# Folding weights in column quarters, loading q, k and v apart, the last tile in halves, and one more batch's q and k transposed by DMA

## Chip, cores and metric

One core of one Trainium2 chip runs the whole program. The metric is the device time of one execution in microseconds (us). The kernel before took 204.28 us (median of 3 runs, 203.37 to 205.15) when the change was proposed, and 204.2 to 204.9 us in every later group of runs.

## The reference

Windowed attention with four sink positions, then a multiplicative feed-forward layer over the 3072 tokens:

```python
# q, k, v: (4, 8, 768, 64) fp32; n_sink = 4, window = 128
scores = q @ k.T / sqrt(64)
keep   = (key < n_sink) | (0 <= query - key < window)
attn   = softmax(where(keep, scores, -1e9)) @ v
x      = attn.transpose(0, 2, 1, 3).reshape(3072, 512)
out    = ((x @ w1) * (x @ w2)) @ w3 @ w_out     # w1, w2: 512x1024, w3: 1024x1024, w_out: 1024x512
```

## The kernel before

The product w3 @ w_out ("the fold", `w3o`) is computed once at the start, while the first loads arrive. Each of the four batches then goes through the same stages: load q, k, v (GpSimd's queue, cast to bf16), transpose q and k, scores, softmax, values, gates (`pg`, the matmuls with w1 and w2), projection (`po`) and store. Batches overlap. The instruction order on TensorE, ScalarE, VectorE and SP is fixed when the program is built, by a small list scheduler inside the kernel which models when each load arrives; GpSimd's order is chosen by the framework.

```python
XPOSE   = (2, 3)        # batches whose q and k are transposed by DMA; 0 and 1 by TensorE
X_XPOSE = (2, 3)        # the same for x
...
qN = per_batch("qN", [P, NB, DM], 2)      # two buffers: batch 3's q overwrites batch 1's
kN = per_batch("kN", [P, NB, DM], 2)
vN = per_batch("vN", [P, NB, H, VS], 3)   # VS = 72
...
def load_qkv(b, kb):                      # one 128-row block: k, q, v in turn
    for src, dst in ((k, heads(kN[b][:, kb, :])), (q, heads(qN[b][:, kb, :])),
                     (v, vN[b][:, kb, :, 0:D])):
        nc.gpsimd.dma_start(out=dst, in_=rows(src, b, kb))
...
def transposes(src, dst, t):              # TensorE: 8 matmuls and a VectorE copy
    ...
def transposes_dma(src, dst, kb):         # SP's queue
    nc.sync.dma_start_transpose(out=dst[:, :, kb * P:(kb + 1) * P], in_=src[:, kb, :])
...
def project(b, m):
    po = ps_mm.tile([P, DM], FP32, tag="mm", name="po")
    ...                                   # 8 matmuls of 512 columns
    o_sb = work.tile([P, DM], FP32, tag="o_sb", name="o_sb")     # pool of 3 buffers
    nc.scalar.copy(o_sb[:], po[:])
    nc.sync.dma_start(out=out[t0:t0 + P, :], in_=o_sb[:])        # SP's queue too
...
# scheduler's constants
MARGIN = {"av": 0.3}; YIELD = {..., "sc": 0.4, ...}
PACE = 5.0              # least us of the model's time between two units of scores
```

The softmax here doesn't subtract the row's maximum and nothing guards it: scores larger than these inputs give would overflow.

## Time and profile before

| | before |
|---|---|
| time, span of the profiled run | 203.94 us, 202.2 us |
| granted TensorE clock | 1.000 |
| first gate matmul | 39.57 us |
| TensorE's waits of over 0.45 us after that | none |
| last matmul ends, tail to the end of the span | 198.6 us, 3.6 us |
| chain of work that ended last | PE 87%, DMA 7% |

A wait is time in which an engine stands idle in front of an instruction; the profile writes it in brackets behind that instruction, with what ended it. TensorE (PE) ends this kernel, so its waits are what matters, and those of other engines only if they come through to it. The prediction shows the page's lines and reads them.

### The profile page before, as it was taken

How to read it: one execution, taken by the hardware profiler on the slowest of the kernel's cores; microseconds unless marked ns; L12 is line 12 of the kernel's file. 1: busy time of each engine (PE TensorE's matmuls, PEld its weight loads, DVE VectorE, ACT ScalarE, POOL GpSimd, SP SyncE). 2: the span in 40 equal slices, each digit the busy share in tenths (PEclk: the TensorE clock that was granted, in tenths of full speed). 3: DMA queues.
4: the chain of work that ended last, by engine and by line, in shares of the span. 5: the costliest groups of instructions: out<-in, count | busy, mean ns of one | idle time of the engine just before them, and what ended most of it. 6: DMA issues, size and time to landing. Idle time of an engine off the chain costs nothing.

```text
span 202.2 us, 4514 instructions
## 1 busy us (share of the span) xinstructions
PE 192.7 (95%) x1800; PEld 120.7 (60%) x1813; DVE 109.9 (54%) x263; ACT 107.0 (53%) x180; POOL 74.1 (37%) x97
## 2 busy tenths in 40 slices
PE   7949899999999999999999999999999999999992
PEld 2425466698886885576666655566665466554440
DVE  4613288665897773467878654877775044440000
ACT  2231556755765866777666664666663433333331
POOL 6699494488999963622770000000000000000000
PEclk9999999999999999999999999999999999999999
DMA  5999999999999999999999994502021610002333
GB/s 154 294 219 173 165 197 206 192 156 154 154 150 151 161 144 126 214 175 204 155 132 157 118 161 129 159 5 52 3 52 67 192 55 2 0 3 104 150 145 120
DMA packets 102773, 27.04 MB, mean 134 GB/s; under 512 B 95072, under 2 KB 98144, under 8 KB 102752
## 3 DMA queue, kind: packets, MB, share of 16 engines
q0 software_dynamic: 78624, 13.64, 91.5%
q1 hardware_dynamic: 24128, 13.11, 29.9%
q8 instruction: 14, 0.23, 0.5%
q14 instruction: 7, 0.06, 0.1%
HBM read 29.36 MB, written 6.29 MB: 176 GB/s over the span
## 4 chain that ended last, share of the span: by engine, by line
PE 87%; DMA 7%; ACT 2%; issue 1%; DVE 1%; SPq 1%; ACTq 0%
PE pg L316 42%; PE po L362 19%; PE av L276 7%; PE sc L245 6%; DMA ab_106<-in_moe_w_dram 5%; PE pw L351 3%; PE tp L191 2%; PE ph L351 2%; DMA xT_104<-xn 2%; PE xt L292 1%; PE pz L376 1%; PE sp L226 1%; ACT w3o L355 1%; SPq L140 1%; ACT w_sb L163 1%
## 5 line engine op out<-in xcount | busy, mean ns | idle before, releaser
L316 PEld LDWEIGHTS <-w_sb 128*128 128x128 bf16 x576 | 53.0, 98 | 25.5 <-issue 1.6
L323 ACT COPY a_sb<-pg 128x384 f32<-128x384 f32 (+1 forms) x72 | 32.0, 445 | 35.2 <-PE pg L316 15.0
L250 ACT ACTIVATE ex<-sc 128x1024 bf16<-128x1024 f32 (+1 forms) x48 | 44.8, 955 | 7.6 <-PE sc L245 7.0
L254 DVE TENSOR_TENSOR am<-ex,maskt 128x1024 bf16<-128x1024 bf16 (+1 forms) x48 | 30.3, 641 | 4.4 <-ACT ex L250 4.2
L366 ACT COPY o_sb<-po 128x512 f32<-128x512 f32 x24 | 14.1, 586 | 26.9 <-PE po L362 26.7
L316 PE MATMUL pg<-xT_102,w_sb 128*128 128x256 bf16 x192 | 24.3, 273 | 0.0
L316 PE MATMUL pg<-xT_103,w_sb 128*128 128x384 bf16 x128 | 23.7, 326 | 0.0
L316 PE MATMUL pg<-xT_104,w_sb 128*128 128x384 bf16 x128 | 22.6, 326 | 0.4 <-DMA xT_104<-xn 0.4
L283 DVE TENSOR_TENSOR xn<-av,rec 128x256 bf16<-128x256 f32 x48 | 20.4, 424 | 4.1 <-DMA xT_104<-xn 2.5
L316 PE MATMUL pg<-xT_105,w_sb 128*128 128x384 bf16 x128 | 21.0, 326 | 0.0
L276 PEld LDWEIGHTS <-am 128*128 128x128 bf16 x352 | 17.0, 97 | 3.3 <-issue 0.3
L320 DVE TENSOR_TENSOR ab_109<-a_sb,pg 128x384 bf16<-128x384 f32 x16 | 8.8, 553 | 17.1 <-PE pg L316 17.1
L280 DVE RECIPROCAL rec<-av 128x4 f32<-128x4 f32 x48 | 8.6, 180 | 16.5 <-PE av L276 16.2
L320 DVE TENSOR_TENSOR ab_106<-a_sb,pg 128x256 bf16<-128x256 f32 x24 | 10.0, 418 | 5.7 <-PE pg L316 4.2
L376 PE MATMUL pz<-ksbd_113 128*128 128x512 bf16 x36 | 10.5, 444 | 1.4 <-DVE ksbd_113 L146 1.3
L362 PE MATMUL po<-w3o,ab_106 128*128 128x512 bf16 x45 | 11.2, 379 | 0.2
L320 DVE TENSOR_TENSOR ab_108<-a_sb,pg 128x384 bf16<-128x384 f32 x16 | 8.9, 554 | 4.4 <-PE pg L316 1.6
L362 PE MATMUL po<-w3o,ab_107 128*128 128x512 bf16 x46 | 10.9, 379 | 0.1
L351 PEld LDWEIGHTS <-w3t 128*128 128x128 bf16 x64 | 6.0, 97 | 8.3 <-issue 2.0
L362 PE MATMUL po<-w3o,ab_108 128*128 128x512 bf16 x46 | 10.6, 379 | 0.1
L362 PE MATMUL po<-w3o,ab_109 128*128 128x512 bf16 x47 | 10.5, 379 | 0.1
L320 DVE TENSOR_TENSOR ab_107<-a_sb,pg 128x384 bf16<-128x384 f32 x16 | 8.8, 552 | 2.7 <-ACT ex L250 1.5
(143 smaller groups left out, 254.4 us busy)
## 6 DMA issues: line engine op xcount, KB each, us to landing
out_dram<-o_sb SPq DMA_DIRECT2D x24, 256.0 KB, 2.1
w_sb<-in_moe_w_dram POOLq DMA_DIRECT2D x5, 512.0 KB, 10.1
ab_106<-in_moe_w_dram SPq DMA_DIRECT2D x2, 512.0 KB, 7.5
w_sb<-in_moe_w_dram POOLq DMA_DIRECT2D x4, 256.0 KB, 8.3
ab_107<-in_moe_w_out_dram SPq DMA_DIRECT2D x2, 512.0 KB, 6.9
kN_86<-in_k_dram POOLq DMA_DIRECT2D x6, 128.0 KB, 8.8
qN_82<-in_q_dram POOLq DMA_DIRECT2D x6, 128.0 KB, 8.6
vN_90<-in_v_dram POOLq DMA_DIRECT2D x6, 128.0 KB, 8.5
```

The lines of the kernel that those rows point to most:

```text
L245: nc.tensor.matmul(sc[:, e, c:c + n], kT[b][hp, r, kb * P:(kb + 1) * P], qT[b][hp, r, qb * P:qb * P + n], start=True, stop=True)
L250: nc.scalar.activation(ex[:, :, c0:], sc[:, :, c0:], ACTF.Exp, scale=scale)
L254: nc.vector.tensor_mul(am[:, :, c0:], ex[:, :, c0:], mk)
L276: nc.tensor.matmul(o, lhs, rhs, start=(n == 0), stop=(n == len(todo) - 1), skip_group_check=True)
L283: nc.vector.tensor_mul(xns[b, t][:, :, r, :, :], av[:, :, :, 0:D], rec[:].to_broadcast([P, 2, 2, D]))
L316: nc.tensor.matmul(pg[:], w_sb[:, kk, dt * P:(dt + 1) * P], xT[b][:, kk, tk], start=(kk == 0), stop=(kk == NP - 1))
L320: nc.vector.tensor_mul(ab[b][:, dt, tk], gate_a.pop((b, c, dt))[:], pg[:])
L323: nc.scalar.copy(a_sb[:], pg[:])
L351: nc.tensor.matmul(po, w3T[i][:, j, :], wo_sb[:, j, :], start=(j == 0), stop=(j == KFF - 1))
L362: nc.tensor.matmul(po[:], ab[b][:, kk, m * P:(m + 1) * P], w3o[:, kk, :], start=(kk == 0), stop=(kk == KFF - 1))
L366: nc.scalar.copy(o_sb[:], po[:])
L376: nc.tensor.matmul(pz[:], idle[:, 0:P], idle[:, 0:512], start=True, stop=True)
```

## The change

The intent is to take work and waits off TensorE: start the fold sooner (in quarters, the first with both ScalarE and VectorE casting), put the first q, k and v where they are wanted, move batch 1's 48 transposing matmuls to DMA, and shorten the tail. The scheduler's constants were re-tuned along with it. Cut to its core:

```diff
-    XPOSE = (2, 3)
+    XPOSE = (1, 2, 3)
...
-    def load_qkv(b, kb):           # k, q, v of a block in turn
+    def load_heads(names, b, kb):  # "kq" or "v"
...
-    order = [('w3', 0, 2, 1, 2), ('w3', 2, 4, 1, 2), ('wo', 1), ('qkv', 0, 0, 2), ...
-             ('qkv', 1, 0, 6), ('qkv', 2, 0, 6), ('qkv', 3, 0, 6)]
+    order = [('wo', 4, 6), ('w3', 0, 2, 512), ('w3', 2, 4, 512), ('wo', 6, 8), ('qk', 0, 0), ...
+             ('qk', 2, 4), ('v', 3, 0), ('qk', 3, 0), ('qk', 3, 2), ('qk', 3, 4), ('v', 3, 2), ('v', 3, 4)]
...
-        for h in range(2 if i < SPLIT else 1):                       # fold in halves
+        parts = [(0, 2), (2, 4), (4, 6), (6, 8)] if i < SPLIT else [(0, KFF)]
...
+    def project_last():            # last tile: two halves of 256 columns, the second
+        ...                        # copied in quarters by VectorE and ScalarE, three stores
-                task(("av", b, r, t), 3, ...)
+                task(("av", b, r, t), 5, ...)
-                task(("p", b, m), 1300 + 200 * b + m, ...)
+                task(("p", b, m), 1380 + 200 * b + m, ...)
-    MARGIN = {"av": 0.3};  YIELD "sc": 0.4;  PACE = 5.0
+    MARGIN = {"av": 0.5};  YIELD "sc": 0.6;  PACE = 2.75
```

## The prediction

> **What bounds the kernel now.** I read the page's first two parts first, then the chain of work that ended last, then the DMA totals of single stretches, and last the timeline around the places that mattered.
>
> ```profile
> span 202.2 us, 4514 instructions
> ...
> PE 192.7 (95%) x1800; PEld 120.7 (60%) x1813; DVE 109.9 (54%) x263; ACT 107.0 (53%) x180; POOL 74.1 (37%) x97
> ...
> PE   7949899999999999999999999999999999999992
> ...
> DMA  5999999999999999999999994502021610002333
> ```
>
> The reader is to see two full rows. TensorE is busy throughout, DMA only to slice 24 or so, some 125 us. TensorE ends the kernel, so what counts is its useful work plus whatever it waits. The chain gives the real spacing of its matmuls (busy means include the pipeline and can't be added):
>
> ```profile
> 43.29 3.49 PE pg L316 x32
> 46.79 0.89 PE tp L191 x16
> ...
> 160.56 20.80 PE pg L316 x128
> 181.62 10.74 PE po L362 x49
> ```
>
> That is 0.109 us for a 256-column matmul, 0.055 for a 128-column one, 0.1625 for 384 and 0.217 for 512. Laying the program's order of TensorE out with these spacings (scores about 0.046 and values about 0.034 apiece, from the same chain) gives 179.9 us of useful work. It starts at 1.3 and ends at 198.6, so some 17.4 us are lost: about 14.5 before the first gate matmul at 39.6 (fillers and waits for loads), 1 before the first gate of batch 2, the rest in small pieces.
>
> The DMA row needs a rate. Two stretches, the first (42 to 57 us) with cast loads alone, the second (70 to 98) with loads, transposes and stores:
>
> ```profile
> q0 software_dynamic: 18023, 2.27, 248.9%
> ```
>
> ```profile
> q0 software_dynamic: 15563, 1.96, 118.1%
> q1 hardware_dynamic: 6836, 2.78, 64.3%
> ```
>
> A q, k or v load writes 0.131 MB, so the first stretch did 17.3 loads in 15 us: 0.87 us a load. In the second, 15 loads take 13.0 of 28 us; the hardware queue moved 5 stores (1.31 MB, about 0.75 us each, 3.7) and 1.47 MB of transposes, 11.2 of them, in the 11.3 us left: **1.0 us a transpose**. Between 98 and 130 us, 12 loads, 18 transposes and 3 stores make 31 of 32 us, which agrees. So DMA is a full server until about 125 us, and each item put in delays what is behind it.
>
> How late were the last batch's q and k?
>
> ```profile
> 98.19 1.19 SPq L200 DMA_TRANSPOSE kT_101<-kN_89  x1
> ...
> 123.98 0.50 PE L245 MATMUL sc<-qT_97,kT_101 64*128 64x256 bf16 x8
> ```
>
> The first transposes of batch 3 go out at 98.2 to 103.9, and their first reader runs at 124.0. Even with some 7 us to land they were early by more than 12 us. That slack is what the change spends.
>
> **What the Trainium skill says.** "DMA: Bandwidth & Descriptors", section "Queues, rings and completion order", says that an engine round-robins between the queue rows that have work. The trace agrees that loads and transposes share: a v load of batch 1 landed in 6.8 us with no transposes about, one of batch 3 in 15.4. The same page, "Issuing engine by pattern", gives plain DMA transposes to the hardware path (SP here): all stand in SP's queue, in order, behind each other and the stores. Its "Latency and other measured facts" has 261 GB/s for a transpose, which for 0.131 MB would be 0.5 us; this trace says 1.0 and I use that. "TensorE: Matmul & The Clock Gate", "The HAM clock gate", says an idle window of about 3.4 us halves the clock until some 3.4 us of work have passed. Before shows slow matmuls only at its start (0.43 us apart in place of 0.217); it has no later gap long enough to test it.
>
> **The change part by part.**
> *Batch 1 transposed by DMA.* Takes 48 transposing matmuls from TensorE: 48 x 0.055 = 2.65 us, on the bounding engine, and six VectorE copies of 0.69 us, which nobody waited for. The useful work becomes 177.3 us. Adds 12 transposes to DMA: 12 x 1.0 = 12 us, in a stretch where it is full.
> *Loads apart and reordered.* Up to the first w2 half (landed at 35.8 before: the load eight places later, which reuses its slot, goes out then) the new order has six more q, k, v loads: 35.8 + 6 x 0.9 = 41.2. But by the first gate TensorE has then 27.3 us of useful work behind it, against 23.8 at 39.6 before; the offset of the clock over work done is 13.9 in place of 15.8. The fold in quarters and the casts on two engines help there (fillers fall from 37 to 26): 1.9 us won at the front, if nothing waits later.
> *Last tile in halves.* Before, TensorE ends at 198.6 and the span at 202.2: a 0.59 us copy, a 256 KB store and the end. Now the last copies are 128 columns wide, on two engines, and the stores 64 KB: about 0.3 + 0.3 us saved. The tail becomes 3.0.
> Sum if nothing waits: 177.3 + 13.9 + 2.5 of small losses + 3.0 = **196.7 us** of span against 202.2, that is 198.6 us of time.
>
> *But the loads' order has a side that the diff doesn't show.* In the built program GpSimd's instruction order for batch 3 is v x2, k x6, v x4, then q x6: all q last (they overwrite q of batch 1, whose transposes now are DMAs that finish late, and the scheduler put the rest ahead). Before, k and q alternated. The first scores of batch 3 need two blocks of q transposed, and TensorE executes in order. When does the first q arrive? In both kernels all weights and batch 0 are in at about 46.8 (from the slot reuse; same bytes). After that come, ahead of or with that q: 49 loads (18 + 18 + 13), 12 + 12 transposes of batches 1 and 2, one k of batch 3 and two x transposes, six stores:
> 49 x 0.87 + 27 x 1.0 + 6 x 0.75 = 42.6 + 27 + 4.5 = 74.1; 46.8 + 74.1 = **120.9**.
> The same sum for before's first k of batch 3: 40 x 0.87 + 12 + 4.5 = 51.3, which gives 98.1; the trace issues its transpose at 98.19. So I trust the sum to a microsecond or two.
> SP's queue then holds q, k, q at about 1.3 us each, the second q going out at about 123.6, and landing takes 2.4 to 9 us in the trace for batch 3; with four loads still about I take 3.5: **127**. TensorE without waits would be there at 102.4 us of work + 13.9 + 1 = 117.3. It waits near 10 us. Then its x transposes for batch 2's gates stand in the same queue behind those: about 1.2 more. A 10 us gap would also cool the clock by what the skill says: about 1.5 more.
> The sum on the path: 127 + (177.3 - 102.4 = 74.9 of work; before took 74.6 us for 73.9, so + 0.7) + 1.2 + 1.5 + 3.0 = 208.3 us of span. Time is about 1.7 to 2 us over the span (203.94 profiled for 202.2): 210. Because I may have the landing and the cooling too high, I say **209**.
>
> **The rivals.**
> *The gain stands* (198 to 200 us): the transposes of batch 1 come from TensorE, DMA's extra 12 us hide. For it: DMA is idle from 130 us on, and before had over 12 us of slack. Against: the q loads move 9 loads (8 us) later on top of the 12, and TensorE gets there 5 us sooner.
> *A wash* (201 to 205): q arrives as I say but a shorter wait, with landing in 2.4 us and no cooling. It takes back just what the front and the 2.65 us won. This is close to my figure and can't be ruled out.
> *Stalls come earlier, too*: batch 2's third pair of transposes lands at about 110 by the same sums, TensorE wants it at about 107. It would not add: the wait at batch 3 is fixed by DMA, and swallows earlier ones.
> *The front gets worse* (fold in quarters with VectorE's memsets in between, raw loads in 1 KB rows): this too would be swallowed, as long as DMA runs as before. So the front hardly matters for the time, if I'm right.
>
> **Range and chances.** The sum has an error of 2 us at the arrival, 2 at the landing, 2 at the cooling: 209 with 203 to 214. Faster by over 2% means under 200.2 and needs the wait to be nearly absent: 0.08. Slower by over 2% is above 208.4: 0.55. Within: 0.37.
>
> **What would show it.** Right: one wait of TensorE of 7 to 12 us for the transposed q of batch 3 at the first scores of batch 3, ending at about 127; SP's transpose of that q held until 120 to 122; DMA's row full to about 140; first gates at about 41 us; about 75 to 78 us from those scores to TensorE's end; tail about 3.0 us; low clock spacing (0.3 us and more) just after the wait. Wrong: q and k of batch 3 in time (a wait under 3 us, and a span of some 197), which would mean that a transpose costs DMA much less than 1.0 us beside loads, or that something earlier on TensorE is the new limit.

## The result, and the profile after

The changed kernel took **210.62 us** (median of 4 runs, 209.94 to 213.54, the last of these in the slow state) against 204.38 (4 runs, 203.37 to 205.15). The ratio is 1.0297, with a 95% interval of 1.0228 to 1.0366: slower. The slow run is left out of the ratio. Ratios here are the mean time of one kernel's fast runs over that of the other's of the same rounds, so not quite the ratio of the medians quoted. The profiled run was fast, at 211.16 us.

The page of the changed kernel, its rows of busy tenths and its chain:

```profile
span 209.4 us, 4456 instructions
PE 191.0 (91%) x1747; PEld 117.8 (56%) x1762; DVE 108.4 (52%) x266; ACT 106.3 (51%) x181; POOL 75.2 (36%) x98
...
PE   7989998999999998699996977499999999999993
...
PEclk9999999999999999699999999999999999999999
DMA  6999999999999999999999995564202330001344
...
PE 52%; DMA 34%; POOL 5%; SPq 4%; issue 2%; DVE 2%; ACT 0%; ACTq 0%; DVEq 0%
```

TensorE's row, unbroken before, now has dents at slices 16, 21 and 23 to 25. A slice is 5.2 us, so these are at about 85, 112 and 120 to 135 us. In slice 16 the clock is low, too. The chain has become a third DMA. The DMA row is full to about 126 us, where it was to about 121 before, so it doesn't show the added work by itself; the last of all loads does, which GpSimd issues at 117.5 us instead of 103.8. TensorE's waits, longest first (total us, times, longest):

```profile
PE pg L324 <- ACT o_sb L374: 5.3, 2, 3.0
PE sc L253 <- DMA qT_97<-qN_85: 2.9, 1, 2.9
PE sp L234 <- DVE am L262: 2.1, 1, 2.1
```

There are four waits of over 2 us, 10.2 us together. TensorE's timeline places three of them (start, duration, instruction, and in brackets the idle time before it):

```profile
85.40 2.72 PE L324 MATMUL pg<-xT_103,w_sb 128*128 128x384 bf16 x8 [2.29 <-ACT o_sb L374]
...
127.18 0.51 PE L253 MATMUL sc<-qT_97,kT_101 64*128 64x256 bf16 x8 [2.91 <-DMA qT_97<-qN_85]
...
134.40 2.76 PE L324 MATMUL pg<-xT_104,w_sb 128*128 128x384 bf16 x16 [2.96 <-ACT o_sb L374]
```

The one at 127.18 is the first scores of batch 3. SP's queue just before it shows why, and also what stood behind:

```profile
110.51 1.21 SPq L208 DMA_TRANSPOSE kT_101<-kN_89  x1
121.80 1.19 SPq L208 DMA_TRANSPOSE qT_97<-qN_85  x1
...
130.02 0.34 SPq L377 DMA_DIRECT2D out_dram<-o_sb  x1
```

Between 111.7 and 121.8 SP issued nothing: the transpose of q at its head waited for a load. The store that left at 130.02 had its tile ready when ScalarE's copy ended at 120.4; it stood behind those transposes. ScalarE's timeline shows what that costs:

```profile
84.76 0.59 ACT L374 COPY o_sb<-po 128x512 f32<-128x512 f32 x1 [3.56 <-DMA out_dram<-o_sb]
...
133.76 0.59 ACT L374 COPY o_sb<-po 128x512 f32<-128x512 f32 x1 [4.64 <-DMA out_dram<-o_sb]
```

ScalarE stood 3.56 and 4.64 us until a store had landed: all three output buffers were full. As its copy did not come, the slot in PSUM (the memory into which TensorE writes) was not freed, and TensorE stood as well, 2.29 and 2.96 us. So the waits at 85 and 134 are waits for stores. The fourth, at 113.76 before `sp`, is put down to a VectorE tile, but `sp` also reads `qT_96`, batch 2's transposed q, whose third pair went out at 104.60 and landed at 113.67 by the trace, just before the wait ended.

Is a transpose still 1.0 us of DMA? From 98 to 121 us, when only loads and transposes moved (q0 are GpSimd's loads, q1 what SP issues; packets, MB, and the time that their packets took as a share of the 23 us in 16 engines, which can pass 100% as packets overlap):

```profile
q0 software_dynamic: 19404, 2.45, 186.9%
q1 hardware_dynamic: 3818, 0.92, 37.1%
```

2.45 MB are 18.7 loads of 0.131 MB, 16.3 us at 0.87 us each; 6.7 us are left for 7.0 transposes, 0.96 us each. The prediction's rate holds.

The tail: TensorE's last matmul, then the two last quarter copies.

```profile
204.08 1.91 PE L387 MATMUL po<-w3o,ab_109 128*128 128x256 bf16 x16
```

```profile
206.41 0.27 ACT L396 COPY o_sb<-po 128x128 f32<-128x128 f32 x1 [1.50 <-DVE o_sb L396]
```

VectorE's copy ran from 206.08 to 206.37, and only then did ScalarE's begin. They were meant to run side by side. The tail is 3.4 us.

### The profile page after: what moved, and what is told of

Same layout as the page of the kernel before. It is cut to its first block, busy times and chain, and to the rows that moved or that the text cites. A ratio compares the mean times of both kernels' runs of the same rounds, so it can differ in the third digit from the quotient of the medians.

```text
span 209.4 us, 4456 instructions
## 1 busy us (share of the span) xinstructions
PE 191.0 (91%) x1747; PEld 117.8 (56%) x1762; DVE 108.4 (52%) x266; ACT 106.3 (51%) x181; POOL 75.2 (36%) x98
## 4 chain that ended last, share of the span: by engine, by line
PE 52%; DMA 34%; POOL 5%; SPq 4%; issue 2%; DVE 2%; ACT 0%; ACTq 0%; DVEq 0%
PE pg L324 28%; PE po L370 11%; DMA vN_92<-in_v_dram 8%; DMA kN_88<-in_k_dram 7%; DMA qN_85<-in_q_dram 6%; DMA kN_89<-in_k_dram 4%; DMA qN_82<-in_q_dram 4%; PE av L284 3%; PE pw L359 3%; PE sc L253 3%; SPq L208 2%; DMA ab_106<-in_moe_w_out_dram 2%; POOL vN_92 L105 2%; DMA out_dram<-o_sb 2%; SPq L311 1%
## 5 line engine op out<-in xcount | busy, mean ns | idle before, releaser
L324 PEld LDWEIGHTS <-w_sb 128*128 128x128 bf16 x576 | 54.5, 98 | 31.0 <-issue 7.6
L262 DVE TENSOR_TENSOR am<-ex,maskt 128x1024 bf16<-128x1024 bf16 (+1 forms) x48 | 29.8, 641 | 3.6 <-ACT ex L258 3.5
L374 ACT COPY o_sb<-po 128x512 f32<-128x512 f32 x23 | 13.5, 587 | 31.9 <-PE po L370 22.3
L324 PE MATMUL pg<-xT_103,w_sb 128*128 128x384 bf16 x128 | 25.0, 339 | 2.3 <-ACT o_sb L374 2.3
L324 PE MATMUL pg<-xT_104,w_sb 128*128 128x384 bf16 x128 | 22.8, 326 | 3.0 <-ACT o_sb L374 3.0
L324 PE MATMUL pg<-xT_102,w_sb 128*128 128x256 bf16 x192 | 22.1, 273 | 0.0
L324 PE MATMUL pg<-xT_105,w_sb 128*128 128x384 bf16 x128 | 21.0, 326 | 0.1
L284 PEld LDWEIGHTS <-am 128*128 128x128 bf16 x352 | 16.2, 97 | 2.5 <-issue 0.8
L328 DVE TENSOR_TENSOR ab_109<-a_sb,pg 128x384 bf16<-128x384 f32 x16 | 8.9, 555 | 15.2 <-PE pg L324 15.2
L328 DVE TENSOR_TENSOR ab_106<-a_sb,pg 128x256 bf16<-128x256 f32 x24 | 10.1, 421 | 10.0 <-PE pg L324 9.8
L370 PE MATMUL po<-w3o,ab_106 128*128 128x512 bf16 x44 | 11.1, 379 | 0.2
L370 PE MATMUL po<-w3o,ab_107 128*128 128x512 bf16 x45 | 10.9, 379 | 0.2
L370 PE MATMUL po<-w3o,ab_108 128*128 128x512 bf16 x46 | 10.4, 379 | 0.1
L359 PEld LDWEIGHTS <-w3t 128*128 128x128 bf16 x64 | 5.4, 97 | 8.7 <-DVE w3t L345 4.0
L359 PE MATMUL ph<-wo_sb,w3t 128*128 128x512 bf16 x31 | 8.3, 380 | 1.6 <-DVE w3t L345 1.1
L405 PE MATMUL pz<-ksbd_113 128*128 128x512 bf16 x24 | 8.6, 508 | 1.3 <-DVE ksbd_113 L151 1.3
```

The lines of the kernel that those rows point to most:

```text
L262: nc.vector.tensor_mul(am[:, :, c0:], ex[:, :, c0:], mk)
L284: nc.tensor.matmul(o, lhs, rhs, start=(n == 0), stop=(n == len(todo) - 1), skip_group_check=True)
L324: nc.tensor.matmul(pg[:], w_sb[:, kk, dt * P:(dt + 1) * P], xT[b][:, kk, tk], start=(kk == 0), stop=(kk == NP - 1))
L328: nc.vector.tensor_mul(ab[b][:, dt, tk], gate_a.pop((b, c, dt))[:], pg[:])
L359: nc.tensor.matmul(po, w3T[i][:, j, :], wo_sb[:, j, :], start=(j == 0), stop=(j == KFF - 1))
L370: nc.tensor.matmul(po[:], ab[b][:, kk, m * P:(m + 1) * P], w3o[:, kk, :], start=(kk == 0), stop=(kk == KFF - 1))
```

## The experiments

The theory after the first look: DMA is the server that is behind; batch 1's transposes delay every later load, and TensorE pays in whatever it then asks for first. The rivals: it is the order of batch 3's loads alone; it is the stores behind transposes alone; it is the new pace, or the new front. All twelve profiled runs were in the fast state. Times are medians of all runs, ratios are of fast runs to the kernel before in the same rounds.

| run | what it is | us | ratio, 95% interval |
|---|---|---|---|
| after | the change | 210.62 | 1.0297 (1.0228 to 1.0366) |
| e1 | after, batch 1 transposed by TensorE | 206.37 | 1.0077 (1.0033 to 1.0122) |
| e2 | before, batch 1 transposed by DMA | 213.48 | 1.0456 (1.0410 to 1.0503) |
| e3 | after, k and q of batch 3 in turn | 206.32 | 1.0103 (1.0051 to 1.0155) |
| e4 | after, stores on ScalarE's queue | 221.26 | 1.0833 (1.0777 to 1.0888) |
| e5 | e1 with the old pace | 205.05 | 1.0012 (0.9989 to 1.0034) |
| e6 | after with the old pace | 217.23 | 1.0627 (1.0580 to 1.0674) |
| e7 | after, four output buffers | 209.41 | 1.0213 (1.0154 to 1.0272) |
| e8 | after, only k of batch 1 by DMA | 211.84 | 1.0368 (1.0328 to 1.0409) |
| e9 | after, 12 v loads left out (wrong result) | 200.67 | 0.9793 (0.9756 to 0.9831) |
| e10 | before, last tile in halves | 204.80 | 0.9996 (0.9976 to 1.0016) |
| e11 | e5 with four output buffers | 204.93 | 1.0005 (0.9985 to 1.0025) |
| e12 | e3 and e7 together | 205.03 | 1.0009 (0.9984 to 1.0035) |

### e1 and e2: the change without the transposes, and the transposes without the change

```diff
 # e1, on after                 # e2, on before
-XPOSE = (1, 2, 3)             -XPOSE = (2, 3)
+XPOSE = (2, 3)                +XPOSE = (1, 2, 3)
```

> The changed kernel, with q and k of batch 1 transposed on TensorE again (XPOSE back to batches 2 and 3); everything else of the change stays. Theory A (DMA is a full server; the twelve added transposes, and the place of batch 3's q behind all other loads, make TensorE wait for batch 3's q): without the twelve the waits of 2.1 and 2.9 us for transposed q, and the two waits of 2.3 and 3.0 us for an output buffer behind them, go; useful work rises by 2.65 us to 179.9. Span 179.9 + 14.5 (front) + 2.5 (small losses) + 3.3 (tail) = 200, time 202, ratio to before 0.98 to 0.995. Rival B (the new load order, pace and fold by themselves bring the waits): time stays above 207.

> The kernel before, with one part of the change alone: q and k of batch 1 transposed by DMA. Theory A: useful work falls to 177.3, but q and k of batch 3 come 12 us later; by the count of loads, transposes and stores ahead of them the first pair lands near 125 where TensorE would be ready at about 122: waits of 3 to 6 us in sum, span 203 to 206, time 205 to 208, ratio 1.00 to 1.02. Rival C (the transposes as such pay, the loss is from the rest of the change or from q being loaded last): below 202, ratio under 0.99.

Both directions came as expected and both sizes were missed. In e2 the transposes alone cost 4.6%, more than the whole change, although k and q of batch 3 are loaded in turn there: the order of these loads alone can't be the cause. Its longest wait, 3.26 us ending at 128.2, runs through yet another buffer: VectorE could not write its next x tile until a transposed x had landed.

```profile
127.13 0.42 DVE L283 TENSOR_TENSOR xn<-av,rec 128x256 bf16<-128x256 f32 x1 [5.28 <-DMA xT<-xn]
```

In e1 the four waits are gone, but a new one of 2.46 us stands at 119:

```profile
119.02 0.29 PE L234 MATMUL sp<-qT,ksbd 128*32 128x256 bf16 x4 [2.46 <-DMA qT<-qN]
```

The reason is in the program's order: with the new pace, and with a model that sees less DMA work, the scheduler puts batch 3's first scores after 94.6 us of TensorE work, where the kernel before has 106.0 and the changed one 102.4. Without the transposes the loads come earlier, and they are asked for earlier still. One more thing moved: in e1 (and e5) GpSimd loads k and q of batch 3 in turn again, so e1 holds e3's cure as well, and what it won can't be put down to the transposes alone.

### e3: only the order of batch 3's loads

```diff
-    for x in order[GATED:]:
-        load(*x)
+    with tc.manual_schedule(engines={mybir.EngineType.Pool}):
+        for x in order[GATED:]:
+            load(*x)
```

The built program differs in GpSimd's order for batch 3 alone, where k and q now alternate.

> The changed kernel with only the order of batch 3's loads put back to k, q, k, q (GpSimd's list held in written order); TensorE's, VectorE's, ScalarE's and SP's orders are the same, all twelve added transposes stay. Theory A: the second q of batch 3 is issued nine loads sooner, near 117 in place of 124; the wait at the first scores of batch 3 (2.9 us) goes, and the 3.0 us wait for an output buffer, whose store stands behind that q in SP's queue, goes too; the waits near 83 and 112 stay. Time 205 to 206, ratio to the changed kernel about 0.975. Rival D (only the sum of DMA work counts, not its order): within 1 us of the changed kernel.

206.32 us, just over the 205 to 206 of the theory and far from the rival. The first q of batch 3 is transposed at 112.09 instead of 121.80, and TensorE no longer waits for it:

```profile
112.09 1.22 SPq L209 DMA_TRANSPOSE qT<-qN  x1
```

```profile
123.97 0.50 PE L254 MATMUL sc<-qT,kT 64*128 64x256 bf16 x8
```

So "all q last" was 1.9 points of the 3.0 (1.0297 to 1.0103). The output-buffer wait that was to go with it only shrank, from 2.96 to 1.91 us. Left are 2.7 us for output buffers, 1.8 for v of batch 2 and 1.7 for q of batch 2.

### e4: the stores out of SP's queue

```diff
-        nc.sync.dma_start(out=out[t0:t0 + P, :], in_=o_sb[:])
+        nc.scalar.dma_start(out=out[t0:t0 + P, :], in_=o_sb[:])
```

> The changed kernel with the output stores (all but the last tile's) issued from ScalarE's queue in place of SP's; the scheduler then also puts batch 3's loads as k, q, k, q. Theory A with the part found in the trace (stores stuck behind transposes that wait for loads hold the three output buffers, ScalarE waits for a buffer, and TensorE for the PSUM slot that ScalarE empties): the waits of 2.3, 2.9 and 3.0 us go, the one of 2.1 us near 112 for q of batch 2 stays or grows to 4, since DMA sets it. Time 203 to 205. Rival: if ScalarE's issue time (0.3 to 0.4 us each, 23 times) delays its copies on the path, 206 or more.

A clear miss, 221.26 us, from one wait: TensorE stood 19.3 us before scores that needed ScalarE to empty earlier ones first (`ex`). ScalarE's timeline:

```profile
88.50 0.38 ACTq L377 DMA_DIRECT2D out_dram<-o_sb  x1
88.98 0.81 ACT L258 ACTIVATE ex<-sc 128x768 bf16<-128x768 f32 x1 [20.58 <-DMA kT<-kN]
```

ScalarE's last work before that ended at 68.4. It then stood in front of a store's issue until a transposed k had landed. The semaphores in the packed trace show why: the DMAs issued by SP and by ScalarE share eight completion semaphores. This store has number 115, as had the transpose of k that SP issued at 80.65 us, and ScalarE waited on 115 until that transpose landed, at 88.42. A queue that can be held does not become harmless by moving it onto a computing engine: the engine is then held with it. (The order of batch 3's loads changed along with it to k and q in turn, as expected.)

### e5 and e6: the old pace

```diff
-PACE = 2.75; MARGIN "av": 0.5; YIELD "sc": 0.6; av prio 5; p prio 1380
+PACE = 5.0;  MARGIN "av": 0.3; YIELD "sc": 0.4; av prio 3; p prio 1300
```

e5 is e1 with this edit, e6 is the changed kernel with it.

> The changed kernel without the transposes of batch 1 by DMA (as in e1) and also with the scheduling constants of the kernel before (pace of the score units 5.0 instead of 2.75, the old priorities of values and projections). Theory: what held e1 back was only the new pace, which asks for batch 3's scores before DMA can deliver them (its one wait of 2.46 us at 119); with the old pace they are wanted some ten us of work later, so no wait of over 1 us stands after 50 us, and the gain of front and tail (about 2 us at the front by my prediction) shows: 200 to 203 us, 0.98 to 0.995 of the kernel before. Rival (the new front and the split loads are no gain on this chip, whatever the pace): 204 or more.

> The changed kernel with its transposes of batch 1 by DMA kept, and the scheduling constants of the kernel before. Theory: the transposes of batch 1 are the cost and the pace only says where it shows; batch 3's scores are wanted later, so the wait that ended at 127.2 goes, but waits for v of batch 2, for x transposes or for output buffers behind the transposes stand in its place: 207 to 213 us (e2, the kernel before with these transposes, took 213.5). Rival (the new pace is the cause of the loss, not the transposes): 201 to 205 us.

e5 took 205.05 us, level with before. The 2.46 us wait did go, as the theory had it, though one of 1.55 us for an output buffer stands at 119; the gain expected from the front did not come, which is the rival's outcome. e6 is even slower than expected, at 217.23 us, so the new pace is not the cause of the change's loss; it had softened it. The waits of e6:

```profile
PE vp L223 <- DMA vN<-in_v_dram: 3.9, 1, 3.9
PE po L370 <- ACT o_sb L374: 3.8, 1, 3.8
PE pg L324 <- ACT o_sb L374: 1.5, 1, 1.5
```

The wait for q of batch 3 is absent here, with the same load order as in the changed kernel; v and the output buffers have taken its place. What is asked for first pays.

### e7: a fourth output buffer

```diff
-    VS = 72
+    VS = 70                       # makes room
-    o_sb = work.tile([P, DM], FP32, tag="o_sb", name="o_sb")
+    o_sb = work.tile([P, DM], FP32, tag="o_sb", bufs=4, name="o_sb")
```

The order of instructions on every engine is that of the changed kernel.

> The changed kernel with four output buffers instead of three (the row of v is padded to 70 instead of 72 to make room); the order of instructions on every engine is unchanged. Theory: the waits of 2.29 us at 85.4 and of 2.96 us at 134.4 are ScalarE waiting for an output buffer whose store stands behind transposes in SP's queue; with a fourth buffer each falls below 1 us. The third q of batch 3 still cannot be transposed before about 122 and lands at about 127, so the wait there grows by what the first gave back, to about 5 us; the net gain is that of the last wait, 2 to 3 us: 207.0 to 209.0 us. Rival (the buffers are the whole cause and their waits add up): 205 us. Rival (the buffers are not the cause): 210.6 us, the waits unchanged.

209.41 us, a little above the 207.0 to 209.0 of the theory; with three fast runs its interval overlaps that of the changed kernel, so in time alone the gain isn't clear of noise. The traces show what happened. Both output-buffer waits are gone. The first one's 2.29 us came back further on: 2.0 us for v of batch 2 at 89.4, and the scores of batch 3 still run at 126.8, after a wait of 3.18 us (5 were expected).

```profile
126.82 0.51 PE L253 MATMUL sc<-qT,kT 64*128 64x256 bf16 x8 [3.18 <-DMA qT<-qN]
...
127.63 2.98 PE L370 MATMUL po<-w3o,ab 128*128 128x512 bf16 x8
...
132.60 2.76 PE L324 MATMUL pg<-xT,w_sb 128*128 128x384 bf16 x16
```

Removing 2.29 us of wait at 85 moved the instruction at 127.18 by 0.36 us. That is what it means for a later wait to swallow an earlier one. From there to the gates that had the last wait took 5.78 us instead of 7.22, so only 1.44 of the 2.96 us was won. The second line shows where the rest went: eight 512-column matmuls took 2.98 us, where eight run in 1.89 at the same place of the changed kernel. The clock was at half from 128.27 to 131.68.

### e8: half the dose

```diff
-                if b in XPOSE:
+                if b in XPOSE and (b > 1 or n == "k"):       # and the same in the scheduler's model
```

> The changed kernel with only k of batch 1 transposed by DMA, q of batch 1 by TensorE: 6 transposes on DMA instead of 12, and 24 transposes back on TensorE (24 x 0.055 = 1.3 us). Theory (the cost is the DMA time of the transposes, about 1 us each in a queue that is full to 125 us): about half of the loss of e1 to the changed kernel (206.4 to 210.6) is given back: 207.5 to 209.5 us. Rival (only the order of the loads of q behind the transposes of q of batch 1 counts; q's buffer is now free early): the wait at batch 3's scores is gone and 205 to 207 us.

A miss for both theories: half the transposes, and 211.84 us, no faster than the changed kernel (1.0368 against 1.0297, with intervals that overlap). The supply did improve (the last load of batch 3 was issued at 113.3 instead of 117.5 us, with two of v now behind q), but this edit also tells the scheduler's model that DMA has less to do, and it asks for batch 3's v after 79.2 us of TensorE work instead of 84.4. The two longest waits are one for that v, and one through VectorE's x tile, as in e2:

```profile
99.22 0.46 PE L223 MATMUL vp<-vN,sel 128*128 128x64 bf16 x8 [3.15 <-DMA vN<-in_v_dram]
...
122.83 1.04 PE L324 MATMUL pg<-xT,w_sb 128*128 128x384 bf16 x4 [3.13 <-DVE xn L291]
```

So e1 and e8 change supply and demand at once and can't measure a dose. e9 was made to change the supply alone.

### e9: supply alone

```diff
+    vN[2], vN[3] = vN[0], vN[1]
...
         if what in ("qk", "v"):
+            if what == "v" and i[0] > 1:
+                return
```

The model still counts these loads, so the instruction order on TensorE, ScalarE, VectorE and SP is exactly that of the changed kernel, there are three output buffers, and q of batch 3 is still last. The result is wrong on purpose.

> The changed kernel with the twelve loads of v of batches 2 and 3 left out (their values are taken from batches 0 and 1, so the result is wrong on purpose); order of instructions on TensorE, ScalarE, VectorE and SP unchanged, and on GpSimd q of batch 3 still comes after all of k of batch 3. It takes 12 x 0.87 = 10.4 us of DMA time away, about what the twelve transposes of batch 1 added. Theory (supply: loads and transposes together keep DMA behind what TensorE asks for, and every one of the four waits comes from a load that lands late): the waits at 85, 114, 127 and 134 us fall to under 1 us each, and the span comes near the sum of my prediction if nothing waits, 196.7 to 199.5: 198 to 202 us. Rival (SP's in-order queue and the load order alone make the waits, DMA's time does not): two waits of 2 us or more stay, 206 us or more.

200.67 us: the theory's figure, and faster than the kernel before. TensorE's waits, longest first:

```profile
PE pz L408 <- DVE ksbd L154: 1.3, 1, 1.3
PE ph L362 <- DVE w3t L348: 1.1, 2, 0.8
PE ph L362 <- DVE wo_sb L193: 0.8, 2, 0.7
PE sp L237 <- DVE qT L205: 0.8, 1, 0.8
PE pg L327 <- ACT o_sb L377: 0.5, 1, 0.5
```

All four are gone, though nothing was done to the load order, the buffers or SP's queue. The first four lines are from the first 34 us; the output buffers cost 0.5 us. Taking 10.4 us of DMA time away was enough for everything: the last load goes out at 103.7 us, as early as before the change. All twelve loads left out stood ahead of batch 3's q in GpSimd's queue, so what this shows is that an earlier supply is enough, in the order as it was.

### e10 and e11: the tail alone, and an attempt to beat both

e10 adds `project_last` to the kernel before; e11 is e5 with e7's four buffers.

> The kernel before with the last tile in halves and nothing else of the change. Theory: the tail after the last matmul hardly shortens, because in the changed kernel the two last quarter copies ran one after the other and the tail was 3.4 us there and 3.6 before: 0.0 to 0.5 us faster, 0.9975 to 1.000 of before. Rival (my prediction's 0.6 us): 0.6 us or more, 0.997 or less.

> As e5 (no transposes of batch 1 by DMA, the old pace), with four output buffers (row of v padded to 70). Attempt at a version that beats both. Theory: e5's one wait of over 1 us (1.55 us at 119, ScalarE held by an output buffer) goes: 1 to 1.5 us faster than e5, 0.993 to 0.997 of the kernel before (about 203.3 us). Rival (the time comes back as a later wait): 0.999 or more.

e10 is a hit: the halves of the last tile are worth nothing that 22 runs can show (0.9996). e11 is a miss: e5's wait of 1.55 us fell to 0.64, but the time stayed at 1.0005. Its first gate has 14.9 us of lost time ahead of it instead of e5's 15.7, so about 1.7 us should have been won; both profiled spans are 203.3. Which small losses took it, these two profiles don't settle. No version here beats the kernel before with a right result.

### e12: both cures

```diff
 # e3's manual_schedule on GpSimd, and e7's VS = 70 with bufs=4
```

> Both cures at once on the changed kernel: GpSimd's loads of batch 3 with k and q in turn (e3) and four output buffers (e7). Theory (DMA supply is the cause, order and buffers only choose where it shows): e3's two waits for output buffers (0.75 and 1.91 us) go, but its waits for v of batch 2 (1.84 us) and the transposed q of batch 2 (1.73 us) stay or grow, so at most half of the 2.7 us is won: 204.5 to 206.5 us, still slower than the kernel before. Rival (the cures add up): 203.5 us or less, level with the kernel before.

205.03 us, within the theory's range in time but not in its claim: it is level with the kernel before (1.0009), not slower. The gain over e3 is 0.9 points, as much as e7 alone gave, so the two cures seem to add, and I had expected at most half. (Neither gain is large beside its interval, and e12 is less steady: five of its 20 runs, 206.1 to 209.0 us, count as slow and are left out.) The waits that are left are supply:

```profile
PE vp L224 <- DMA vN<-in_v_dram: 2.6, 2, 1.5
...
PE sp L235 <- DVE am L263: 1.2, 1, 1.2
```

### The sum of it

One point is about 2.05 us.

| step | ratio | points |
|---|---|---|
| the change | 1.0297 | |
| batch 3's q in turn with k (e3) | 1.0103 | -1.9 |
| and a fourth output buffer (e12) | 1.0009 | -0.9 |
| or, in place of both, 10.4 us of DMA time less (e9) | 0.9793 | -5.0 from the change |

The gain that the change aimed at, about 2%, is there once DMA isn't late; e9 shows it. DMA's lateness eats it and 3% more. Of these 5.0 points, order and buffers alone give back 2.9 (1.94 and 0.94). The other 2.2 are a difference between two runs that weren't built on each other; e12's waits suggest that they are mostly loads that simply aren't there yet.

## Why the prediction was right

The time (209.0 predicted, 210.62 measured), the range and the direction were right.

- **DMA's arithmetic: right where it was asked.** The transpose of batch 3's first q was to be issued at 120.9 and went at 121.80; the wait at the scores was to end at 127 and ended at 127.18. The 1.0 us per transpose came out as 0.96. Two of its readings don't hold. "31 of 32 us" for 98 to 130 us before is no check: the trace gives DMA a share of only 0.58 from 121 to 130 us; with DMA busy for some 27 of the 32 us, as the row of that stretch gives, a transpose there comes to about 0.8 us (an estimate). And DMA's row was not full to 140 us: from 126 to 140 its share is 0.56.
- **One wait of about 10 us: wrong in form, right in sum.** This is the step that failed. It was 2.9 us at that place, and 10.2 us in four. TensorE was to come there at 117.3 and came at 124.27, held up by earlier waits of 4.35 us and a low clock. I had one earlier stall in view (batch 2's third pair, 2.06 us at 113.76) and said that it would be swallowed, which held. The waits for output buffers I had not seen: I had SP's queue down for "about 1.2" us behind the transposes, for x. It was stores that stood there, and they cost 2.96 us after the scores. The 2.29 us ahead of them was swallowed (e7: 0.36 us came through).
- **After the scores: right by luck.** From them to TensorE's end I had 78.3 us in the sum, and it took 78.8. But in it were 1.2 us for x and 1.5 for cooling, 2.7 together, which did not come; the wait of 2.96 us for an output buffer took their place.
- **Cooling: wrong in place.** I put 1.5 us of low clock just after the wait at 127. There the clock was full. It was low from 85.06 to 88.47, after 2.29 us, where it too was swallowed. In e7, with a wait of 3.18 us at the scores, the low clock came and cost 1.5 us (2.96 less 1.44). The length of a wait doesn't decide it. After the start, every low clock in these traces lasts 3.41 us (in e4 six times that). Cut each trace into stretches of 3.41 us, counted from where its clock first is full, and every low clock starts on one of these cuts. The changed kernel's stretch before its low clock, and the low one (length, TensorE's busy time, ..., granted clock, DMA share, GB/s):

```profile
81.65:85.06 3.41, 1.46 (x34) 1.18 (x33) 1.41 (x5) 0.30 (x1) 2.36 (x4) 1.00 1.68 210
85.06:88.47 3.41, 3.07 (x13) 1.73 (x13) 0.94 (x2) 2.18 (x4) 1.37 (x2) 0.50 1.76 159
```

TensorE was idle for 1.95 us of the first (matmul ends are modelled). In the traces of all runs, from 40 us to TensorE's end, each stretch with 1.95 us idle or more was followed by a low one, and none with 1.85 or less was, but for one in e2 (1.33 us idle, among short matmuls). The 2.91 us before 127.18 lay across a cut, 1.80 us of idle time in the stretch before it and 1.16 after; of e7's 3.18 us, 1.97 lay in one stretch. The cuts lie elsewhere in each run (the clock is first full between 4.31 and 7.25 us), so where a low clock falls is partly chance.

- **The sum if nothing waits: 196.7 predicted, 198.7 in e9.** The terms that were mis-sized are the front and the tail. The first gate ran at 41.77 us with 27.3 of work behind it, an offset of 14.5, not 13.9; in e9 it was 15.2 and in e1 and e5 15.9 and 15.7, against 15.8 before. So "1.9 us won at the front" is 0 to 1.5 (e7, at 41.55 us, is the earliest). The tail is 3.4 and not 3.0, as the two last copies ran in turn. That leaves 2.8 for small losses (2.5 foreseen): 177.3 + 15.2 + 3.4 + 2.8 = 198.7. (The spacing of 0.217 holds, though 10.74 over 49 is 0.219: matmul records can be missing, and lines of eight in 1.73 us give 0.216.)
- **The rivals.** "The gain stands" fell, and e9 shows what it would have needed: 10 us less of DMA work. "A wash" is what the change becomes with both cures (e12). "The front hardly matters for the time" held for the changed kernel, where 127 is set by DMA, but not in e5, where nothing waits for a load any more and the front still gave nothing.

Not foreseen at all: that the same lateness would show up through v, x tiles or output buffers as soon as q is on time. That late supply is the cause is shown by e9 against the changed kernel, with every other engine's order fixed, and by e2 against before and e6 against e5, where the transposes cost 4.6 and 6.2 points at the old pace. How much of the loss is to be put down to the load order or the buffers depends on what else is changed: e3 and e12 show that these decide where, and how much of, the lateness is paid. Open are why ScalarE's last copy waits for VectorE's, and where e11's expected gain went.

## What to carry to other kernels

Before moving work from the bounding engine to DMA, sum DMA's time up to the moment the result is wanted; a queue that is full until then hands every added microsecond to what comes after it, whatever the average load. Where stores share an in-order queue with transfers that wait for loads, count the output buffers as part of that path. To measure a supplier, change the supply with the consumer's order fixed: an edit that a scheduler also sees moves the demand too, and can hide what was to be measured.

## What the Trainium skill lacked or had wrong

- "DMA: Bandwidth & Descriptors", "Latency and other measured facts": its 261 GB/s for a transpose gives 0.5 us for 0.131 MB; beside cast loads these traces give 0.96 to 1.0 us of DMA time (estimates, from stretches in which DMA was full), and 8 us from issue to landing while the queue is full.
- "TensorE: Matmul & The Clock Gate", "The HAM clock gate": an idle window of about 3.4 us. The 3.41 us fit these traces as the length of each low clock, but far less idle time is enough: 1.95 to 2.02 us within one such stretch (changed kernel, e6, e7 twice), while waits of 2.46 (e1), 2.91 and 2.96 us that lay across two stretches were not followed by a low clock.
- None of the pages gives a figure for what a held transpose costs the plain stores behind it in the same issuing queue: 10.1 us without an issue on SP, and up to 4.64 us of ScalarE waiting for a free output buffer.
- None has e4's case: a plain store on ScalarE's queue that shares its completion semaphore with a transpose on SP's waits until that transpose has landed, 20.58 us of idle time on ScalarE.
